# First expert layer: rest blocks of at most 64 rows get a TensorE unit of their own, in line ahead of the 128-row unit

## The chip, the cores and the metric

The kernel runs on one core of one Trainium2 chip. The metric is the device time in microseconds (us) from start to end of one execution; the median of the runs counts. Engines are named as the profile names them: PE is TensorE (PEld its weight loads), DVE is VectorE, ACT is ScalarE, POOL is GpSimd, SP is SyncE. A q behind an engine's name (PEldq, DVEq) stands for its instruction sequencer, which handles branches, registers and semaphore waits.

## What is computed

Retention attention, then two mixture-of-experts layers with one expert per token. Cut to what matters here:

```python
def _moe_ref(x, w_gate, w_output_gate, w1, w2):      # N, D, E, F = 4608, 512, 8, 1024
    e_idx = np.argmax(x @ w_gate, axis=1)
    for e in range(E):
        mask = e_idx == e
        h = np.maximum(x[mask] @ w1[e], 0.0)
        ye = h @ w2[e]
        out[mask] = gate_w[mask, None] * eom[mask, e, None] * ye

def reference(**kwargs):
    x = _attn_ref(q, k, v)                           # 8 x 8 heads, 576 rows, 64 wide
    x = _moe_ref(x, ...)                             # the first layer
    return _moe2_ref(x, ...)                         # the second, gated with a modality bias
```

On the inputs of the reference, its gate gives the eight experts of the first layer 602, 613, 589, 549, 586, 487, 608 and 574 rows. In the second layer two experts get all rows (2315 and 2293).

## The kernel before

Attention and routing of the first layer come first, in an order written out by hand (a plan sorted by numbers). The rows of each expert are scattered into a region of their own in DRAM. Then `experts` runs sixteen places in turn, 0 to 7 for the experts of layer one and 8 to 15 for those of layer two. Every engine has its own instruction stream, with branches on registers, and the streams meet only in semaphores: `take(engine, name)` waits for a semaphore and takes from it (its line in the profile is L547).

An expert's rows are worked in units. A unit of slot 0 or 1 is a pair, 256 rows. What is left is one rest unit (s = 2). The registers `np` (pairs) and `od` (the rest) are made in `counts` from the row count n of each expert: `np` is (n + 127) >> 8, and `od` was ((n + 127) >> 6) & 2, so 2 for a rest of 1 to 128 rows and 0 otherwise (a rest above 128 rows counts as a pair). By the counts above, every expert of layer one has two pairs; experts 0, 1, 2, 3, 4, 6 and 7 have a rest unit, with 90, 101, 77, 37, 74, 96 and 62 rows, and expert 5 has none.

What a unit does on each engine:

- PE, stage one (`quarter`, L1136 to L1138): four quarters of the hidden layer, 24 matmuls each, with the weights `w1` loaded and the rows `xT` moving. A pair moves 256 columns per matmul, a rest unit 128 (`cs = cols(P_, w)`). Each quarter gives `ph_full`.
- ACT (`relus`, L1264) makes the high half of `hT` from the quarter in `ph` and gives `hh_full`; DVE (`rests`, L1388) makes the low half and gives `h_full`.
- PE, stage two (`second`, L1144 to L1146): 24 matmuls per block of 128 rows, with `hT` loaded and 512 columns of `w2` moving. It takes `h_full` once before every six matmuls. `py_full` ends it.
- ACT and DVE (`back`): the squares and the scale of the block (`sq`, `eb`), then its two halves for the next layer (`x2row`). ACT and DVE run `back` of a unit before `relus` and `rests` of the next unit.
- Routing of the second layer runs one unit behind: PE's `logits` (L1114) and `ranks` (L1119, L1120), DVE's `choose` (the last step writes `oh`) and `place`. In a rest unit PE computes the logits of the previous pair's first block after six matmuls of stage two, and waits for `oh` at the end of stage two before the ranks.

The order within one expert of layer one is written by `walk`: the branches on `np` and `od` stand between the units. `co.jump(reg, op, value, target)` is a compare and branch that is taken to `target` or falls through; it has the line of the helper, L669. Branches inside units (`when`) have L648. After a rest unit comes `co.to(after)`, and then the next expert's first pair.

In layer two `walk` already chooses between a rest unit of 128 columns (`od` is 2) and one of 64 columns (`SMALL`, `od` is 1). `cols` gives a small unit of layer one the first 64 columns, and one of layer two the last 64.

## Time and profile before

| | |
|---|---|
| median of 3 runs | 987.47 us (987.39 to 988.93) |
| the profiled execution's own time | 986.25 us |
| its span, first to last instruction | 984.5 us |
| PE busy | 964.9 us, 98% of the span |
| DVE, ACT, POOL busy | 437.1, 353.8, 213.1 us |

The profiled execution takes 1.75 us beside its span and is 1.22 us below the median of the runs shown. A busy PE is one with a matmul in flight: a matmul's shown duration is longer than its distance to the next one, so pace is read from the starts of matmuls, and not from their durations.

### The profile page before, as it was taken

Reading aid. Unit: us, or ns where it says so; the run is one execution under the profiler, and the core shown is the slowest. Engines: PE = TensorE matmul, PEld = TensorE weight load, DVE = VectorE, ACT = ScalarE, POOL = GpSimd, SP = SyncE. Lnnn points to the kernel's source line nnn. Section 1 sums busy time; section 2 is a strip of 40 time slices with the busy share of each in tenths; the row PEclk is TensorE's granted clock in tenths of the full one; section 3 lists DMA queues with packets and bytes.
Section 4 is the critical chain, followed back from the end, with each engine's and each line's share of the span. In section 5 each row is a group of like instructions: output and inputs, shape, how many; then the busy total and the mean of one; then the engine's idle time right before and its main releaser. Section 6 shows DMA issues by size and latency. Waiting matters only on the chain. (4 is left out here: it accounts for less than half of the span.)

```text
span 984.5 us, 25261 instructions
## 1 busy us (share of the span) xinstructions
PE 964.9 (98%) x9218; PEld 684.2 (69%) x9218; DVE 437.1 (44%) x1402; ACT 353.8 (36%) x699; POOL 213.1 (22%) x301
## 2 busy tenths in 40 slices
PE   8999998999999999999999999999999999999997
PEld 6888887666676766767775776776666667766664
DVE  4676677366656565656566663243111211121111
ACT  4665565235444352434453432232111111211111
POOL 6677765011111111111111111100010101000110
PEclk9999999999999999999999999999999999999999
DMA  9999992578376664748664852642221311112101
GB/s 349 375 337 328 330 303 111 121 216 235 75 194 139 150 189 122 196 110 236 121 184 97 235 161 61 215 87 44 55 60 36 76 35 55 43 43 64 54 21 36
DMA packets 170070, 145.20 MB, mean 147 GB/s; under 512 B 135081, under 2 KB 135245, under 8 KB 169936
## 3 DMA queue, kind: packets, MB, share of 16 engines
q1 hardware_dynamic: 160928, 114.85, 43.0%
q0 software_dynamic: 8960, 28.62, 7.8%
q8 instruction: 73, 1.20, 0.5%
q14 instruction: 61, 0.50, 0.2%
q10 hardware_dynamic: 48, 0.04, 0.0%
HBM read 80.46 MB, written 33.92 MB: 116 GB/s over the span
## 5 line engine op out<-in xcount | busy, mean ns | idle before, releaser
L1138 PE MATMUL ph<-xT,wb 128*128 128x256 f16 (+2 forms) x1312 | 329.3, 262 | 0.0
L1137 PE MATMUL ph<-xT,wb 128*128 128x256 f16 (+2 forms) x1312 | 329.3, 262 | 0.0
L1136 PE MATMUL ph<-xT,wb 128*128 128x256 f16 (+2 forms) x1312 | 329.2, 262 | 0.0
L1388 DVE SCALAR_TENSOR_TENSOR hT<-ph,hT 128x512 f16<-128x512 f32 (+2 forms) x164 | 103.2, 636 | 322.0 <-DVEq L547 321.2
L1144 PE MATMUL py<-wb,hT 128*128 128x512 f16 x608 | 230.3, 379 | 0.1
L1146 PE MATMUL py<-wb,hT 128*128 128x512 f16 x608 | 230.4, 379 | 0.0
L1145 PE MATMUL py<-wb,hT 128*128 128x512 f16 x608 | 230.4, 379 | 0.0
L1264 ACT ACTIVATE hT<-ph 128x512 f16<-128x512 f32 (+2 forms) x164 | 90.1, 550 | 175.8 <-ACTq L547 175.6
L1136 PEld LDWEIGHTS ph<-xT,wb 128*128 128x128 f16 x1312 | 128.2, 98 | 15.6
L1137 PEld LDWEIGHTS ph<-xT,wb 128*128 128x128 f16 x1312 | 128.2, 98 | 15.4
L1138 PEld LDWEIGHTS ph<-xT,wb 128*128 128x128 f16 x1312 | 128.3, 98 | 12.2
L1146 PEld LDWEIGHTS py<-wb,hT 128*128 128x128 f16 x608 | 59.4, 98 | 71.8
L1551 POOL DMA_INDIRECT out_dram<-yo,idxo x37 | 35.9, 970 | 334.5 <-POOLq L547 324.7
L1144 PEld LDWEIGHTS py<-wb,hT 128*128 128x128 f16 x608 | 59.3, 98 | 64.3 <-issue 0.9
L1145 PEld LDWEIGHTS py<-wb,hT 128*128 128x128 f16 x608 | 59.4, 98 | 63.2
L559 DVE SCALAR_TENSOR_TENSOR wb<-stg,wb 128x2048 f16<-128x2048 f32 x36 | 82.4, 2288 | 10.0 <-DVEq L547 9.0
L1255 ACT ACTIVATE yo<-py,v_gcol 128x512 f32<-128x512 f32 x37 | 25.4, 687 | 167.5 <-ACTq L547 167.5
L1540 POOL TENSOR_SCALAR idx<-v_pos 128x1 int32<-128x1 f32 x39 | 9.1, 232 | 335.0 <-POOLq L547 335.0
L1238 ACT ACTIVATE wb<-stg 128x2048 f16<-128x2048 f32 x36 | 68.4, 1901 | 0.9 <-ACTq L547 0.9
L1249 ACT ACTIVATE sq<-py 128x512 bf16<-128x512 f32 x39 | 23.3, 596 | 93.4 <-ACTq L547 93.4
L1544 POOL DMA_INDIRECT xs<-x2row,idx x39 | 43.3, 1111 | 37.8 <-POOLq L547 36.5
L332 POOL TENSOR_SCALAR_AFFINE_SELECT a<-a 128x512 f32<-128x512 f32 x64 | 39.5, 641 | 26.2 <-ACT a L326 25.3
(165 smaller groups left out, 946.5 us busy)
## 6 DMA issues: line engine op xcount, KB each, us to landing
stg<-in_moe_w_dram SPq DMA_DIRECT2D x36, 1024.0 KB
dq<-in_dq_dram SPq DMA_DIRECT2D x34, 512.0 KB
vk<-in_vk_dram SPq DMA_DIRECT2D x30, 512.0 KB
w0s<-in_moe_w_dram SPq DMA_DIRECT2D x8, 512.0 KB
xs<-zero SPq DMA_DIRECT2D x8, 262.0 KB, 2.3
xs<-zero SPq DMA_DIRECT2D x8, 258.0 KB
vk<-in_vk_dram SPq DMA_DIRECT2D x8, 256.0 KB
gx<-in_scales_dram SPq DMA_DIRECT2D x5, 256.0 KB
```

The source lines that it names most:

```text
L332: nc.gpsimd.affine_select(out=d4, in_=d4, pattern=[[0, 4], [1, C]], compare_op=ALU.is_ge, fill=0.0, base=0, channel_multiplier=-1)
L559: r = fn(*a, **kw).then_inc(self.sem, 1)
L1136: pe.matmul(o, w1(P_, 0)[:, c, fs], xT[s][:, c, cs], start=(c == 0), stop=False)
L1137: pe.matmul(o, w1(P_, 0)[:, c, fs], xT[s][:, 4 + c, cs], start=False, stop=False)
L1138: m = pe.matmul(o, w1(P_, 1)[:, c, fs], xT[s][:, c, cs], start=False, stop=(c == 3))
L1144: pe.matmul(py[b], hT[:, 0, f, bs], w2(P_, 0)[:, f, :], start=(f == 0), stop=False)
L1145: pe.matmul(py[b], hT[:, 0, f, bs], w2(P_, 1)[:, f, :], start=False, stop=False)
L1146: m = pe.matmul(py[b], hT[:, 1, f, bs], w2(P_, 0)[:, f, :], start=False, stop=(f == 7))
L1238: ac.activation(wb[P_ % 2][:, 0, 2048 * c:2048 * c + 2048], stg[:, 2048 * c:2048 * c + 2048], AF.Copy, scale=WS).then_inc(T["cv_full"])
L1264: ac.activation(hT[:, 0, 2 * g:2 * g + 2, cs], ph[g][:, :, cs], AF.Relu).then_inc(T["hh_full"])
L1388: stt(hT[:, 1, 2 * g:2 * g + 2, cs], ph[g][:, :, cs], 0.0, hT[:, 0, 2 * g:2 * g + 2, cs], op0=ALU.max, op1=ALU.subtract).then_inc(T["h_full"])
L1544: po.indirect_dma_start(out=xs2, out_offset=bass.IndirectOffsetOnAxis(ap=idx[b], axis=0), in_=x, in_offset=None, bounds_check=E * R - 1, o ...
```

## The change

`counts` keeps two bits of the shifted count instead of one and takes one from them (with 0 kept): `od` is now 0 for no rest unit, 1 for a rest of 1 to 64 rows and 2 for 65 to 128. By the counts above experts 3 (37 rows) and 7 (62 rows) get 1; experts 0, 1, 2, 4 and 6 keep 2, and expert 5 keeps 0. All engines but PE still ask only whether `od` is 0, and do for 1 what they do for 2. PE alone is called with `short=True`.

```diff
         nc.vector.tensor_scalar(reg[:, 0:8], c2[:, 0], 8, None, op0=ALU.logical_shift_right)
-        nc.vector.tensor_scalar(reg[:, 8:16], c2[:, 0], 6, 2, op0=ALU.logical_shift_right, op1=ALU.bitwise_and)
+        nc.vector.tensor_scalar(c2[:, 0], c2[:, 0], 6, 3, op0=ALU.logical_shift_right, op1=ALU.bitwise_and)
+        nc.vector.tensor_scalar(reg[:, 8:16], c2[:, 0], 1.0, 1.0, op0=ALU.max, op1=ALU.subtract)
...
-    def walk(co, R_, P_, unit, none=None, conv=None, first=None, late=None, opening=None, owed=None):
+    def walk(co, R_, P_, unit, none=None, conv=None, first=None, late=None, opening=None, owed=None, short=False):
...
             unit(P_, 1, PAIR, True, 1)
-            co.to(block)
+            if short:
+                co.jump(od, "EQ", 0, after)
+                co.jump(od, "EQ", 2, block)
+                unit(P_, 2, SMALL, False)
+                eng.br(after)
+                co.at(block)
+            else:
+                co.to(block)
             if late:
                 co.unlikely(od, "EQ", 0, late, after)
             else:
                 co.jump(od, "EQ", 0, after)
             unit(P_, 2, FULL, False)
             co.to(after)
...
-                    walk(co, R_, P_, unit, none, opening=opening)
+                    walk(co, R_, P_, unit, none, opening=opening, short=True)
```

On PE, at the end of a pair of slot 1 (the last rows of its stage two), the program before goes on to one branch and the 128-column unit:

```order
L1144 MATMUL py<-wb,hT 128x512
L1145 MATMUL py<-wb,hT 128x512
L1146 MATMUL py<-wb,hT 128x512
L679 UNCONDITIONAL_BRANCH
L669 COMPARE_AND_BRANCH
L1136 MATMUL ph<-xT,wb 128x128
L1137 MATMUL ph<-xT,wb 128x128
L1138 MATMUL ph<-xT,wb 128x128
```

The changed program has at the same place two branches and the 64-column unit, whose matmuls have L1144 to L1146 in its own line numbers (stage two is L1152 to L1154 there):

```order
L1152 MATMUL py<-wb,hT 128x512
L1153 MATMUL py<-wb,hT 128x512
L1154 MATMUL py<-wb,hT 128x512
L670 COMPARE_AND_BRANCH x2
L1144 MATMUL ph<-xT,wb 128x64
L1145 MATMUL ph<-xT,wb 128x64
L1146 MATMUL ph<-xT,wb 128x64
```

So a 64-column unit is reached by falling through both branches, and a 128-column unit now by a taken branch that passes the whole 64-column unit.

At the end of the 64-column unit, behind the last matmuls of its stage two, the ranks and the register operation that notes the unit, the changed program leaves by a branch (L779) and has the 128-column unit behind it:

```order
L1154 MATMUL py<-wb,hT 128x512
L1127 MATMUL pr<-oh,tri 128x8
L1128 MATMUL pr<-cum,ones 128x8
L840 ISA
L779 UNCONDITIONAL_BRANCH
L670 COMPARE_AND_BRANCH
L1144 MATMUL ph<-xT,wb 128x128
L1145 MATMUL ph<-xT,wb 128x128
```

So a taken branch now stands between the end of a 64-column unit and the next expert, and it passes the 128-column unit: 140 matmuls with as many weight loads.

On DVE the counts get one more small operation on eight numbers, ahead of the low halves (L456) of the first unit, which is worked before the places begin. Before:

```order
L477 TENSOR_SCALAR c_3275<-cf 1x8
L478 TENSOR_SCALAR reg<-c_3275 1x8
L479 TENSOR_SCALAR reg<-c_3275 1x8
L456 SCALAR_TENSOR_TENSOR hT<-ph_early_3050,hT 128x512
L456 SCALAR_TENSOR_TENSOR hT<-ph_early_3194,hT 128x512
```

And now:

```order
L477 TENSOR_SCALAR c_3275<-cf 1x8
L478 TENSOR_SCALAR reg<-c_3275 1x8
L479 TENSOR_SCALAR c_3275<-c_3275 1x8
L480 TENSOR_SCALAR reg<-c_3275 1x8
L456 SCALAR_TENSOR_TENSOR hT<-ph_early_3050,hT 128x512
```

Nothing else moves on DVE, and no instruction is added, removed or moved on ACT, POOL and SP.

## Rows read from the trace of the kernel before

**Rows 1.** Busy time by engine, whole span.

```profile
PE 964.9 (98%) x9218; PEld 684.2 (69%) x9218; DVE 437.1 (44%) x1402; ACT 353.8 (36%) x699; POOL 213.1 (22%) x301
```

**Rows 2.** Groups by form, PE, 205 to 600 us: count, busy us, mean ns.

```profile
L1138 PE MATMUL ph<-xT,wb 128*128 128x128 f16 x224 | 37.9, 219 | 0.0
```

**Rows 3.** Timeline of PE, rest unit of expert 3: start us, duration us.

```profile
378.60 0.22 PE L1136 MATMUL ph<-xT,wb 128*128 128x128 f16 x1
...
383.96 0.38 PE L1144 MATMUL py<-wb,hT 128*128 128x512 f16 x1
...
389.39 0.27 PE L1136 MATMUL ph<-xT,wb 128*128 128x256 f16 x1
```

**Rows 4.** Timeline of PE, rest unit of expert 7.

```profile
583.17 0.22 PE L1136 MATMUL ph<-xT,wb 128*128 128x128 f16 x1
...
588.53 0.38 PE L1144 MATMUL py<-wb,hT 128*128 128x512 f16 x1
```

**Rows 5.** Timeline of PE, the 64-column unit of layer two.

```profile
782.05 0.19 PE L1136 MATMUL ph<-xT,wb 128*128 128x64 f16 x1
...
784.85 0.38 PE L1144 MATMUL py<-wb,hT 128*128 128x512 f16 x1
```

**Rows 6.** Timelines of ACT, then DVE, from the end of expert 3's second pair.

```profile
378.88 0.60 ACT L1249 ACTIVATE sq<-py 128x512 bf16<-128x512 f32 x1 [3.19 <-ACTq L547]
...
381.01 0.38 ACT L1264 ACTIVATE hT<-ph 128x256 f16<-128x256 f32 x1
...
381.33 0.74 DVE L559 SCALAR_TENSOR_TENSOR x2row<-py,v_s,x2row 128x512 f16<-128x512 f32 x1
382.75 1.12 DVE L1388 SCALAR_TENSOR_TENSOR hT<-ph,hT 128x256 f16<-128x256 f32 x3 [0.68 <-DVEq L547]
```

**Rows 7.** Timeline of DVE at expert 7's rest unit.

```profile
587.32 0.42 DVE L1388 SCALAR_TENSOR_TENSOR hT<-ph,hT 128x256 f16<-128x256 f32 x1 [0.67 <-DVEq L547]
```

**Rows 8.** PE's branches of `jump`: ns min/median/max, first and last start us.

```profile
L669 PEldq COMPARE_BRANCH  x15: 66/75/81, 209.9 to 460.4; - x15
...
L669 PEldq COMPARE_BRANCH  x2: 76/1595/3114, 481.8 to 485.1; - x2
...
L669 PEldq COMPARE_BRANCH  x1: 76/76/76, 387.9 to 387.9; - x1
```

**Rows 9.** PE's branches of `when`, leaving layer two's loops.

```profile
L648 PEldq COMPARE_BRANCH  x2: 75/219/363, 779.0 to 779.4; - x2
...
L648 PEldq COMPARE_BRANCH  x2: 348/1948/3547, 974.5 to 974.9; - x2
```

**Rows 10.** Timeline of PE, end of expert 5's second pair, start of expert 6.

```profile
485.43 0.38 PE L1146 MATMUL py<-wb,hT 128*128 128x512 f16 x1
485.64 0.27 PE L1136 MATMUL ph<-xT,wb 128*128 128x256 f16 x1
```

**Rows 11.** Timelines of PE and DVE at expert 1's first pair.

```profile
232.41 0.27 PE L1137 MATMUL ph<-xT,wb 128*128 128x256 f16 x1
232.52 0.27 PE L1138 MATMUL ph<-xT,wb 128*128 128x256 f16 x1
234.40 0.17 PE L1119 MATMUL pr<-oh,tri 128*128 128x8 f16 x1 [1.60 <-PEq L547]
...
233.91 0.29 DVE L559 TENSOR_SCALAR oh<-w_w,v_m,cur 128x8 f16<-128x8 f32 x1
```

**Rows 12.** Stretches: length, busy us of PE, PEld, DVE, ACT, POOL, granted clock, DMA.

```profile
235.90:239.40 3.50, 3.35 (x18) 2.12 (x16) 2.95 (x3) 1.06 (x1) 2.48 (x3) 0.51 1.01 391
...
8.00:12.00 4.00, 4.00 (x54) 2.85 (x54) 0.99 (x5) 1.47 (x3) 3.27 (x4) 1.00 1.03 389
```

**Rows 13.** Timeline of PE, a pause near the start.

```profile
7.93 1.16 PE L287 MATMUL pa<-dq 64*128 64x128 f32 x16 [2.15 <-DMA dq<-in_dq_dram]
```

**Rows 14.** Timeline of DVE at the counts.

```profile
173.13 0.15 DVE L479 TENSOR_SCALAR reg<-c 1x8 int32<-1x8 int32 x1
...
175.84 0.69 DVE L456 SCALAR_TENSOR_TENSOR hT<-ph_early,hT 128x512 f16<-128x512 f32 x1 [1.36 <-ACT hT L453]
```

## The prediction

> **What bounds the kernel now.** I read the page first, for the busy shares, and see PE busy for 98% of the span and no other engine above half [rows 1]. PE is the bound, so the question is what PE does in a rest unit, and what it would wait for if its part got shorter. Then the groups by form: 224 matmuls of 128 columns on each of three lines are seven rest units of layer one (32 per line and unit) [rows 2], as the row counts say. Two of these, experts 3 and 7, become 64-column units. Then I read PE's timeline at both. Stage one of expert 3's unit runs from 378.60 to 383.96, stage two and the rest of the unit until 389.39, where the next expert's pair starts [rows 3]; expert 7's stage one runs from 583.17 to 588.53 [rows 4]. In both it takes 5.36 us without a pause. So PE itself is what ends last in this stage, but how closely ACT and DVE follow has to be read from their own timelines.

> **Stage one gets shorter.** Layer two has one unit of 64 columns with the same 96 matmuls: 782.05 to 784.85, 2.80 us [rows 5]. The difference, 5.36 - 2.80 = 2.56 us, is what a short unit could give, 5.12 us for two.

> **What PE waits for then.** Stage two needs the first `h_full`, that is DVE's low half of the first quarter. DVE comes to it only behind `back` of the previous pair's second block, whose sums start when that pair's stage two has ended (378.60): ACT's squares at 378.88, its first high half at 381.01, DVE's `x2row` at 381.33, and the first low half at 382.75 [rows 6]. None of this depends on how long PE's stage one lasts, since quarter 0 was there long before, and DVE's order is not changed. A low half takes 0.42 us (the unmerged row at expert 7, [rows 7]), so the first is done at 383.17. From DVE's end to PE's start I take 0.20 us, from another place where PE stood waiting for DVE: `oh` ended at 233.91 + 0.29 = 234.20, and PE started at 234.40 [rows 11]. So stage two can start at 383.37 and not at 381.40, and the gain is 383.96 - 383.37 = 0.59 us. For expert 7 the low half starts at 587.32 [rows 7], so 587.32 + 0.42 + 0.20 = 587.94 against 588.53, again 0.59 us. Sum: 1.18 us faster. The bounds are a hand-over that costs nothing (0.79 us per unit) and one so late that today's start just meets it (0 us). I take 0.59, since PE's hand-over from the same engine is a direct row. The later three low halves follow 0.35 us apart or less (three in 1.12 us, [rows 6]) while stage two asks for one every six matmuls of 0.22 us [rows 10], so they hold nothing up. Stage two and its routing move as they are: the logits are PE's own, and `choose` follows them.

> **The branches.** Fifteen of PE's `jump` branches up to expert 5's pairs, all of which fell through, took 66 to 81 ns. The one that skipped expert 5's missing unit took 3114 ns [rows 8]. It cost nothing on the array: PE's sequencer was at that branch at 481.8 while matmuls already issued ran until 485.64, where the next pair started on pace, 0.21 us behind the last one [rows 10]. The cover was 3.84 us. Skips out of layer two's loops took 363 ns (779.0), 348 ns (974.5) and 3547 ns (974.9) [rows 9]. So of four taken skips of about a unit's length two were dear; I take one chance in two, and 3.11 us as the price.

> [...]

> Five long units (experts 0, 1, 2, 4, 6) now start with a taken branch past the short unit, at the same place as expert 5's skip, with the same cover of 3.84 us. One more branch of 0.08 us stands ahead. I take 0, up to 0.43 us each if a fetch is as slow as the 3547 ns row (2.2 us for five). Expert 5's skip gets longer; I take it as dear as before and as well hidden.

> The return from a short unit has less cover. It stands just ahead of the next expert's branch, which PE's sequencer reached at 387.9 [rows 8], because it had to wait for `oh` before the ranks. The next pair started at 389.39 [rows 3], so the lead was 1.5 us. At expert 6 the same branch at 485.1 [rows 8] was followed by its pair at 485.64 [rows 10], so at most 0.54 us of the lead is needed and at least 0.95 us is slack. A dear return then loses 3.11 - 1.5 = 1.6 to 3.11 - 0.95 = 2.2 us; I take 1.9. A cheap one loses nothing. Two returns at one chance in two: one dear is the likeliest.

> **The operation on DVE.** About 0.15 us like its neighbours. Behind it DVE sat idle for 1.36 us, waiting for ACT [rows 14]; that idle time hides it. Without it, it would cost its 0.15 us.

> **Sum.** -1.18 + 1.9 = +0.7 us against the profiled execution's own 986.25, so 987.0; the same against the median, 987.47, which lies 1.22 above it: **988.2 us**. I count 0.2% (2.0 us) as what a measurement of this kernel can tell from no change, so this is no change.

> **The rivals.**
> - Both returns cheap: only the 1.18 us remain, 986.3 us. For it: the two cheap skips. Against it: expert 5's skip has the same length.
> - Both returns dear: -1.18 + 3.8 = +2.6, 990.1 us. [...]
> - The clock falls, and this one ends slower: PE stands still in each short unit from 378.60 + 2.80 = 381.40 to 383.37, 1.97 us. [...] Two units: 2 x (1.7 - 0.59) = +2.2, 989.7 us. It decides from the first fall of the clock behind a short unit's pause; one fall alone gives +0.5. Against it: a pause near the start, 2.15 us until 7.93 [rows 13], was followed by full clock from 8 to 12 [rows 12], so a pause of this length need not bring a fall. A slow stage two would also cover part of a dear return, so I don't add them.
> - The whole 5.12 us: 982.3 us. It needs low halves that are ready at 381.4. Against it stands DVE's row at 382.75, for which I see no way around.

> **How the numbers follow.** One return dear 0.40 (988.2); both cheap 0.19 (986.3); both dear 0.17 (990.1); the clock falls 0.18 (989.7); the whole gain 0.04 (982.3); long units pay for their skips 0.02 (up to 990.4 with the likeliest case). Faster by over 0.2%: the whole gain and a little for the noise, 0.06. Within: the first two, 0.58 after the noise. Slower: both dear, the clock and the long units, 0.36. The range reaches from both cheap with the gain's upper bound (987.47 - 2 x 0.79 = 985.9) to both dear (990.1, with some room 990.3). The likeliest case's own range, with returns of 1.6 to 2.2 and gains of 0 to 0.79 per unit, is 987.5 to 989.7.

> **What would show it.** Two lots of 96 matmuls of 128x64 in layer one, in 2.8 us each. Behind each a pause on PE of about 2 us, ended by DVE, with stage two starting about 4.8 us behind the pair's end, not 5.36. The `jump` branches of five long units at about 3 us or 75 ns with PE on pace behind them either way. Behind each short unit, either PE on pace or a gap of some 1.9 us before the next expert's first matmul. The granted clock at 1.00 in the 5 us behind each pause. I would be wrong if DVE's first low half came earlier than 4.1 us behind the pair's end, if the clock fell, or if a pause appeared ahead of a long unit.

## The result, and the profile after

| | before | after |
|---|---|---|
| median, us | 987.43 (6 runs) | 997.38 (6 runs) |
| profiled execution, us (its span) | 986.25 (984.5) | 998.05 (996.2) |

The changed kernel takes 1.0101 of the time before (95% interval 1.0091 to 1.0112). That is slower by 10 us, outside the predicted range.

PE stays the bound. This is the line of engines on the page of the kernel after, beside [rows 1]; the second line is the instruction queue q8 from the page's third part (packets, MB, share), which had 73 packets before. (The other instruction queue, q14, has 61 packets in both kernels; it is PE's program that grew, so q8 is taken to be PE's.)

```profile
PE 966.5 (97%) x9218; PEld 682.7 (69%) x9218; DVE 437.1 (44%) x1403; ACT 353.0 (35%) x699; POOL 212.2 (21%) x301
...
q8 instruction: 80, 1.31, 0.6%
```

PE is busy for only 1.6 us more in a span that is 11.7 us longer: the short units take work off it, something puts work time back on, and the rest is standing still. The timeline of PE after, at expert 3's short unit and the start of expert 4's first pair, answers to [rows 3]:

```profile
378.82 0.19 PE L1144 MATMUL ph<-xT,wb 128*128 128x64 f16 x1
...
381.60 0.19 PE L1146 MATMUL ph<-xT,wb 128*128 128x64 f16 x1
383.54 0.38 PE L1152 MATMUL py<-wb,hT 128*128 128x512 f16 x1 [1.75 <-PEq L548]
...
388.97 0.27 PE L1144 MATMUL ph<-xT,wb 128*128 128x256 f16 x1
...
389.30 0.27 PE L1144 MATMUL ph<-xT,wb 128*128 128x256 f16 x1
393.74 0.37 PE L1145 MATMUL ph<-xT,wb 128*128 128x256 f16 x1 [4.17 <-issue]
```

Up to 388.97 this is the forecast: stage one in 2.8 us, a pause of 1.94 us, stage two 4.72 us behind the unit's start in place of 5.36. Then the next pair starts on pace, does four matmuls, and stands still for 4.33 us beyond its pace. "issue" says that PE waited for nothing that the profile shows: no semaphore, no engine, no transfer of data. DVE's timeline has the first low half where the first step put it, 4.15 us behind the unit's start ([rows 6] had 4.15):

```profile
382.97 1.45 DVE L1396 SCALAR_TENSOR_TENSOR hT<-ph,hT 128x256 f16<-128x256 f32 x4 [0.68 <-DVEq L548]
```

At expert 7 the gap stands in front of the pair that follows, and is put down to PE's sequencer (beside [rows 4]):

```profile
590.78 0.19 PE L1144 MATMUL ph<-xT,wb 128*128 128x64 f16 x1
...
593.55 0.19 PE L1146 MATMUL ph<-xT,wb 128*128 128x64 f16 x1
595.72 0.38 PE L1152 MATMUL py<-wb,hT 128*128 128x512 f16 x1 [1.98 <-PEq L548]
...
601.12 0.17 PE L1128 MATMUL pr<-cum,ones 128*128 128x8 f16 x1
604.21 0.27 PE L1144 MATMUL ph<-xT,wb 128*128 128x256 f16 x1 [2.92 <-PEq L548]
```

The branches of PE's sequencer after, beside [rows 8]: the two returns (ns min/median/max, first and last start), then `jump` at expert 5's and expert 6's unit.

```profile
L779 PEldq COMPARE_BRANCH  x2: 281/2295/4309, 387.3 to 599.4; - x2
...
L670 PEldq COMPARE_BRANCH  x1: 4071/4071/4071, 488.5 to 488.5; - x1
...
L670 PEldq COMPARE_BRANCH  x2: 66/1736/3406, 532.9 to 533.0; - x2
```

Expert 7's return took 4309 ns. Expert 3's took 281 ns and looks harmless; its price stands four matmuls later. Over 387.2 to 391.2 us the transfers show no packet of the instruction queue, over 391 to 393 us one:

```profile
q8 instruction: 1, 0.02, 3.0%
```

So no packet was moving while PE worked off the first four matmuls, and PE goes on 1.5 us behind the end of that packet (it ran from 391.31 to 392.27).

The clock comes on top. Stretches of PE after, beside [rows 12] (length, busy us of PE, PEld, DVE, ACT, POOL, granted clock, DMA share, GB/s): behind expert 3's pause, behind expert 3's return, behind expert 7's pause, behind expert 7's return.

```profile
383.50:388.50 5.00, 4.96 (x31) 2.37 (x32) 2.33 (x10) 0.60 (x3) 0.00 (x0) 1.00 0.88 173
392.90:399.70 6.80, 5.96 (x36) 4.30 (x36) 0.92 (x5) 0.84 (x3) 0.00 (x0) 0.50 0.83 249
...
595.70:600.70 5.00, 4.98 (x31) 2.38 (x31) 2.49 (x10) 0.60 (x3) 0.00 (x0) 1.00 0.59 125
604.55:607.90 3.35, 3.35 (x18) 2.41 (x16) 0.00 (x0) 0.00 (x0) 0.00 (x0) 0.50 1.02 139
```

The granted clock stays at 1.00 behind both pauses and is 0.50 behind both returns. In the second stretch PE was busy for 5.96 us; by the starts of its matmuls the clock of 0.50 cost 2.8 us of them.

The account, by the starts of the same stages in the two traces:

| place | us against before |
|---|---|
| up to expert 3's unit | +0.2 |
| the two short units (pause included) | -0.65, -0.42 |
| return from expert 3: the gap, and the clock behind it | +4.3, +2.8 |
| expert 5's skip, now over two units | +0.7 |
| experts 6 and 7, small waits | +0.2 |
| return from expert 7: the gap, and the clock behind it | +3.1, +1.7 |
| sum | +11.9 |

The sum is that of the two profiled executions, of which the one before lies 1.2 us below its kernel's median and the one after 0.7 us above; between the medians it is 10 us.

### The profile page after: what moved, and what is told of

Same layout as the page of the kernel before. It is cut to its first block, busy times and chain, and to the rows that moved or that the text cites. A ratio compares the mean times of both kernels' runs of the same rounds, so it can differ in the third digit from the quotient of the medians.

```text
span 996.2 us, 25276 instructions
## 1 busy us (share of the span) xinstructions
PE 966.5 (97%) x9218; PEld 682.7 (69%) x9218; DVE 437.1 (44%) x1403; ACT 353.0 (35%) x699; POOL 212.2 (21%) x301
## 5 line engine op out<-in xcount | busy, mean ns | idle before, releaser
L1144 PE MATMUL ph<-xT,wb 128*128 128x256 f16 (+2 forms) x1312 | 326.4, 262 | 3.4 <-PEq L548 3.4
L1146 PE MATMUL ph<-xT,wb 128*128 128x256 f16 (+2 forms) x1312 | 326.5, 262 | 0.0
L1152 PE MATMUL py<-wb,hT 128*128 128x512 f16 x608 | 230.3, 379 | 3.7 <-PEq L548 3.7
L1154 PE MATMUL py<-wb,hT 128*128 128x512 f16 x608 | 230.4, 379 | 0.0
L1144 PEld LDWEIGHTS ph<-xT,wb 128*128 128x128 f16 x1312 | 128.3, 98 | 20.3 <-issue 4.2
L1146 PEld LDWEIGHTS ph<-xT,wb 128*128 128x128 f16 x1312 | 128.4, 99 | 17.3 <-issue 4.3
L1154 PEld LDWEIGHTS py<-wb,hT 128*128 128x128 f16 x608 | 59.4, 98 | 71.8
L1152 PEld LDWEIGHTS py<-wb,hT 128*128 128x128 f16 x608 | 59.3, 98 | 67.7 <-issue 4.3
L1548 POOL TENSOR_SCALAR idx<-v_pos 128x1 int32<-128x1 f32 x39 | 7.1, 181 | 347.0 <-POOLq L548 347.0
```

The costliest lines, as they stand in the source:

```text
L1144: pe.matmul(o, w1(P_, 0)[:, c, fs], xT[s][:, c, cs], start=(c == 0), stop=False)
L1146: m = pe.matmul(o, w1(P_, 1)[:, c, fs], xT[s][:, c, cs], start=False, stop=(c == 3))
L1152: pe.matmul(py[b], hT[:, 0, f, bs], w2(P_, 0)[:, f, :], start=(f == 0), stop=False)
L1154: m = pe.matmul(py[b], hT[:, 1, f, bs], w2(P_, 0)[:, f, :], start=False, stop=(f == 7))
```

## The experiments

Theory A: the loss is a wait for instructions behind the short units' return, where nothing covers it, and the clock that falls behind that gap. Rival B: the pause for `h_full` drags the clock down. Rival C: the skips ahead of the long units cost it. The two kernels with fixed units hold the widths of experts 3 and 7 for the counts of this input alone. The absolute times in the first four expectations start from 987.4 us; beside these runs the kernel before took 983.62 us, so it is the differences that are compared. There is one trace of each kernel.

### Short units in place, fixed when the program is built

```diff
-            unit(P_, 2, FULL, False)
+            unit(P_, 2, SMALL if short and P_ in (3, 7) else FULL, False)
```
(and no unit in front of it)

> Experts 3 and 7 get the 64-column unit when the kernel is built (these inputs' counts), in place of the long one; no branch is added and no code is skipped. Theory A (the loss is the wait for instructions behind the return from a short unit, and the clock that falls after it): a pause of about 1.95 us in each short unit stays, no gap behind it, no fall of the clock behind it; 1.2 us under the kernel before, 986.3 us. Rival B (the pause for the first low half is what makes the clock fall): the clock falls behind the pauses as it does in the changed kernel, 3 to 5 us lost, 989 to 991 us. Rival C (the skips ahead of the long units cost the time): as A, no loss.

Measured: 981.64 against 983.62 us, 0.9983 (0.9973 to 0.9992). PE at expert 3, then the stretches behind both pauses:

```profile
378.67 0.19 PE L1139 MATMUL ph<-xT,wb 128*128 128x64 f16 x1
380.62 0.38 PE L1145 MATMUL py<-wb,hT 128*128 128x512 f16 x1 [1.75 <-PEq L548]
...
380.60:385.60 5.00, 4.98 (x31) 2.40 (x32) 2.31 (x10) 0.59 (x3) 0.00 (x0) 1.00 0.90 165
584.70:589.70 5.00, 4.97 (x31) 2.40 (x32) 2.52 (x10) 0.60 (x3) 0.00 (x0) 1.00 0.55 114
```

The same pause, and the clock stays at 1.00: B falls. Without branches the short columns are a gain, and of the size that the prediction gave them (1.18 us of the sum; here 1.7, interval 0.8 to 2.7, and in the trace 0.65 us at each of the two units).

### The copy alone: the unit in front does 128 columns too

```diff
-                unit(P_, 2, SMALL, False)
+                unit(P_, 2, FULL, False)
```

> The branches and the code of the change, but the unit in front works 128 columns like the long one, so that nothing gets shorter and PE doesn't pause for the first low half. Theory A: the returns of experts 3 and 7 each cost a gap of 3 to 4.4 us, and some falls of the clock remain: 5 to 10 us over the kernel before, 993 to 997 us. Rival B: without the pause the clock doesn't fall and the loss is at most the 3 us of one return, 987 to 991 us. Rival C: the whole loss is there, 997 us.

Measured: 993.69 against 983.62 us, 1.0114 (1.0095 to 1.0132). PE behind the two returns:

```profile
386.04 0.27 PE L1144 MATMUL ph<-xT,wb 128*128 128x256 f16 x1
389.92 0.37 PE L1145 MATMUL ph<-xT,wb 128*128 128x256 f16 x1 [3.61 <-issue]
...
596.88 0.17 PE L1128 MATMUL pr<-cum,ones 128*128 128x8 f16 x1
599.91 0.27 PE L1144 MATMUL ph<-xT,wb 128*128 128x256 f16 x1 [2.87 <-PEq L548]
```

No column is saved and no pause is left, and the whole loss is there, with the granted clock at 0.50 from 389.29 and from 600.91 for 3.4 us each. The layout alone (1.0114) and the columns alone (0.9983) multiply to 1.0097, beside 1.0101 for both. The loss belongs to the program's layout, not to the narrower unit. It is 10.1 us, at the upper end of A's 5 to 10 and as much as C expects, so its time speaks against B alone; its trace puts 9.7 us at the two returns, and the next run settles C.

### Skips only: every rest unit long, the copy in front never entered

```diff
-        nc.vector.tensor_scalar(reg[:, 8:16], c2[:, 0], 1.0, 1.0, op0=ALU.max, op1=ALU.subtract)
+        nc.vector.tensor_scalar(reg[:, 8:16], c2[:, 0], 2, None, op0=ALU.bitwise_and)
```

> The short unit's code stands in line, but the rest register is made as before (0 or 2), so all seven rest units are long and are reached by the taken branch past the short one; nothing returns over code but expert 5's skip of both units. Theory A: the branches of 2 to 4 us stand under matmuls already issued, expert 5's skip shows 0.7 us: 987.4 to 988.5 us. Rival B: the same. Rival C: most of the loss is here, 993 to 997 us.

Measured: 984.68 against 983.62 us, 1.0013 (1.0002 to 1.0024). All of it stands at expert 5, whose skip now passes two units (4416 ns):

```profile
483.56 0.38 PE L1154 MATMUL py<-wb,hT 128*128 128x512 f16 x1
484.78 0.27 PE L1144 MATMUL ph<-xT,wb 128*128 128x256 f16 x1 [0.85 <-PEq L548]
```

C is worth 1.0 us, and A expected up to 1.1. The long units' own skips, up to 3431 ns, left PE on pace.

### The long unit in front, the short one behind it

```diff
-                co.jump(od, "EQ", 2, block)
-                unit(P_, 2, SMALL, False)
+                co.jump(od, "EQ", 1, small)
+                unit(P_, 2, FULL, False)
                 eng.br(after)
+                co.at(small)
+                unit(P_, 2, SMALL, False)
...
```

> The long unit stands in front of the short one: five long units fall in and return over the short unit's code, two short units are reached by a taken branch and run on into the next expert. Theory A: five returns instead of two, each 3 to 4.4 us and some with a fall of the clock of 1.7 us: 15 to 28 us over the kernel before, 1002 to 1015 us. Rival B: the two pauses cost what they do in the changed kernel, 994 to 998 us. Rival C: two skips instead of five, under 992 us.

Measured: 998.91 against 983.62 us, 1.0157 (1.0131 to 1.0182). Now five long units return over the short one. PE's five returns, and the gaps behind those of experts 1, 2, 4 and 6:

```profile
L781 PEldq COMPARE_BRANCH  x5: 390/417/6397, 222.9 to 549.7; - x5
...
286.88 0.28 PE L1150 MATMUL ph<-xT,wb 128*128 128x256 f16 x1 [1.05 <-issue]
...
341.03 0.28 PE L1148 MATMUL ph<-xT,wb 128*128 128x256 f16 x1 [1.25 <-issue]
...
450.27 0.37 PE L1148 MATMUL ph<-xT,wb 128*128 128x256 f16 x1 [5.02 <-PEq L548]
...
553.72 0.27 PE L1148 MATMUL ph<-xT,wb 128*128 128x256 f16 x1 [2.52 <-PEq L548]
```

The kernel is 15.3 us above the one before, just inside A's 15 to 28 but not by A's count of five dear returns: three of five took some 0.4 us, and two of these three were followed by an "issue" gap 2 to 3 us into the next pair. Two were dear, with a fall of the clock at each, and expert 5's skip lost 1.2 us. The short units, which return from nowhere here, have no gap behind them. A branch's own duration does not tell its price.

### Low halves early: can the pause go?

The fixed short units again. Besides, ACT and DVE do the unit's first two high and low halves inside the eviction of the pair's last block.

```diff
+                        if held:
+                            back(1, 1, lambda: some(range(2), False))
...
                     ch(ve.reciprocal, v1["inv2"][b], v1["rinv2"][b])
+                    if between:
+                        between()
                     take(ve, "x2h_full")
```
(and the same on ACT, between `sq` and the high half of `x2row`)

> The short units of experts 3 and 7 sit in the place of the long ones, fixed when the program is built, as in the run with the static units (0.9983 of the time before); besides, ACT and DVE do the first two high and low halves of these two units inside the eviction of the pair's last block, where they waited for each other, and not behind it. If the pause of PE in a short unit (1.84 us lost, twice) is only the late first low half, as the sum's first step has it, it is gone: stage two follows stage one on pace, and the run is 2 x 1.84 = 3.7 us faster than the static units, about 5.1 us (0.9948) faster than before. The rival: the eviction's later half, pushed back, is what the next wait is for (the routing of the block, or the buffer that the next pair needs), and the pause moves instead of going: about 0.9983 again, with a new gap of 1 to 2 us behind the unit.

Measured: 981.69 against 986.72 us, 0.9952 (0.9938 to 0.9966). PE around the start of stage two, then DVE:

```profile
381.70 0.19 PE L1139 MATMUL ph<-xT,wb 128*128 128x64 f16 x1
381.98 0.38 PE L1145 MATMUL py<-wb,hT 128*128 128x512 f16 x1
...
381.21 0.76 DVE L1406 SCALAR_TENSOR_TENSOR hT<-ph,hT 128x256 f16<-128x256 f32 x2
...
381.94 0.74 DVE L560 SCALAR_TENSOR_TENSOR x2row<-py,v_s,x2row 128x512 f16<-128x512 f32 x1
```

The first low halves stand ahead of `x2row`, stage two starts 0.28 us behind stage one, and no wait comes in its place. The whole gain is real: 4.7 us (0.9952 of 986.72), where the prediction worked out 5.12. This is also a second run of PE's program of the fixed short units, and expert 5's skip took 3057 ns where it took 3054: the same program showed the same branch time in two traces.

### One stage two for both widths

```diff
...
+                co.jump(od, "EQ", 2, wide)
+                unit(P_, 2, SMALL, False, part=1)
+                eng.br(both)
+                co.at(wide)
+                unit(P_, 2, FULL, False, part=1)
+                co.to(both)
+                unit(P_, 2, FULL, False, part=2)
...
```

> Only stage one of a rest unit exists twice; both widths go on into one common stage two, with its routing, so that nothing returns from a short unit into the next expert. A short unit branches in its middle, over the long stage one, where PE then stands still for DVE for 1.95 us anyway; a long unit skips the short stage one at its head, where 3.84 us of matmuls are queued. Theory A (the loss is the instruction wait behind the return, uncovered, and the clock behind the gap): no gap at the next experts' first pairs, at most a longer pause in the middle of the short units (a wait of 3 to 4.3 us less a cover of about 2.4: 0.6 to 1.9 us each); 0.999 to 1.003 of the time before, with a fall of the clock only if a pause reaches some 3 us. The rival (any short unit reached by a branch costs what the change cost): 1.010 again.

Measured: 988.16 against 986.72 us, 1.0014 (1.0005 to 1.0023). PE inside expert 3's short unit, and behind expert 5's skip (5462 ns):

```profile
383.70 0.38 PE L1158 MATMUL py<-wb,hT 128*128 128x512 f16 x1 [1.76 <-PEq L548]
...
487.39 0.27 PE L1150 MATMUL ph<-xT,wb 128*128 128x256 f16 x1 [1.89 <-PEq L548]
```

No return into the next expert, and no gap there. A branch of 1767 ns in the middle of expert 3's short unit was hidden under its pause. Both short units gain 0.65 us; expert 5's skip takes 2.06 us back. A held, in its range.

### The short unit out of line, at the end of PE's program

```diff
+                co.unlikely(od, "EQ", 1, lambda: unit(P_, 2, SMALL, False), after)
```
(in place of the unit in front)

> The short units stand far behind, at the end of PE's program; the long ones stay in line with no branch around them other than the old skip where there is no rest, and one more branch that falls through. Theory A by distance (what is not just ahead in the program must be fetched, however far): the jump out is covered by the queued matmuls (3.84 us), or loses up to 0.5 us, and the two returns into the next experts lose 3 to 4.3 us each and a fall of the clock each as in the changed kernel: 1.008 to 1.011 of the time before, and expert 5's skip back to what it cost before. The rival (the price hangs on the length of the code that is jumped over): the far jumps cost more than in the changed kernel, over 1.011, with gaps over 5 us.

Measured: 991.12 against 986.72 us, 1.0043 (1.003 to 1.0056). PE in the two short units:

```profile
378.96 0.19 PE L1139 MATMUL ph<-xT,wb 128*128 128x64 f16 x1
382.78 0.19 PE L1140 MATMUL ph<-xT,wb 128*128 128x64 f16 x1 [3.62 <-issue]
...
588.31 0.20 PE L1139 MATMUL ph<-xT,wb 128*128 128x64 f16 x1 [2.20 <-issue]
```

Both theories missed. The jumps out (3632 and 4068 ns) were followed by gaps of 3.8 and 2.4 us inside the short units, which swallowed the pauses; behind the second the clock fell (0.50 from 589.2 to 592.6), for 0.8 us more. Both returns, over far more code, cost nothing on PE. So distance alone does not make a return dear; two returns are too few to say more. Expert 5's skip went back to 2913 ns and was hidden again.

### Work added as cover: 16 matmuls of 512 columns ahead of the return

```diff
+                    if w == SMALL and P_ < E:
+                        for n in range(16):
+                            pe.matmul(ph[3], K["ones"], K["ones"].unsqueeze(1).to_broadcast([P, 4, P]), start=True, stop=True)
```

> The changed kernel with work added: 16 matmuls of 512 columns on constants (16 x 0.21 = 3.4 us) at the end of each short unit, ahead of its return, into sums that nobody reads any more. Theory A: they are the cover that the return lacked, so that the gaps in front of the next experts' pairs (4.3 and 3.0 us) shrink to 1 us or less and the clock no longer falls behind them (it cost 2.8 and 1.7 us): the two places cost 2 x 3.4 in place of 11.9 us, and the kernel with more work is 4 to 5 us faster than the changed one, 1.005 to 1.006 of the time before. The rival (the wait starts only when PE gets to the next pair, or comes from something else than the return): the gaps stay as they are and the kernel is 6.8 us slower than the changed one, about 1.017.

Measured: 1004.06 against 986.72 us, 1.0172 (1.0157 to 1.0188). That is the rival's number, but not by the rival's mechanism. PE behind expert 3's return, the stretches behind both returns, and then expert 6's first pair, behind expert 5's skip:

```profile
395.92 0.27 PE L1144 MATMUL ph<-xT,wb 128*128 128x256 f16 x1 [1.50 <-PEq L548]
...
395.90:400.90 5.00, 4.98 (x52) 4.51 (x53) 1.25 (x6) 1.19 (x4) 0.00 (x0) 1.00 0.86 231
611.70:616.70 5.00, 4.96 (x52) 4.50 (x53) 1.25 (x6) 1.19 (x4) 0.00 (x0) 1.00 0.86 103
...
494.26 0.27 PE L1144 MATMUL ph<-xT,wb 128*128 128x256 f16 x1 [1.86 <-PEq L548]
...
498.68 0.37 PE L1144 MATMUL ph<-xT,wb 128*128 128x256 f16 x1 [3.60 <-issue]
```

At the returns A's mechanism is there: with the added work included they cost 5.1 and 3.9 us, against 7.1 and 4.7 without it, the gaps shrink to 1.7 and 0.5 us (A had 1 or less), and the clock stays at 1.00. The loss moved elsewhere. Expert 5's skip, which passes a longer unit (5434 ns), lost 2.0 us, then 3.8 us more inside the pair, then the clock: 7.2 us in place of 0.7. Some 1.9 us more stand ahead of the first rest unit, where no theory has a claim. The total alone would have told the wrong story.

### PE's program shifted by 128 and by 64 instructions

```diff
+                        if (P_, slot, at) == (0, 1, 5):
+                            with when(pe, was, "EQ", 7):
+                                for n in range(64):
+                                    pe.matmul(ph[3], K["ones"], K["ones"].unsqueeze(1).to_broadcast([P, 4, P]), start=True, stop=True)
```
(range(32) in the second; the branch around them is always taken)

How much of a packet that is, is an estimate from the trace of the kernel before: from 16.2 to 161.4 us it has 22 packets of q8 with 0.36 MB, and 2715 matmuls with 2711 weight loads on PE, so 16.4 KB and 247 of these instructions to a packet, some 66 bytes each, and 128 are about half a packet.

> The changed kernel, with 64 matmuls that are never executed (128 instructions with their weight loads, half of a 16 KB packet of the instruction queue at 64 bytes each) behind a branch in expert 0's second pair, so that all of PE's program behind them lies half a packet further, and nothing else differs. Theory A, as it now stands (an instruction wait comes where PE's sequencer, behind a taken branch, comes to the end of what has been fetched): the same branches are at other distances from the packets' ends, so that the places and the sizes of the gaps change: the 4.3 us gap one matmul behind expert 3's return is gone or elsewhere, and the time differs from the changed kernel's by over 2 us, anywhere between 0.998 (no gap) and 1.017. The rival (the price of a return is fixed by the branch and its distance): the same gaps at the same places, 1.010 within 0.002.

> As the run before it, with 32 matmuls that are never executed: a quarter of a packet. Theory A: again other places and sizes, between 0.998 and 1.017, and of the two shifted kernels at least one differs from the changed one by over 2 us. The rival: 1.010 within 0.002.

Measured: 995.67 and 994.53 against 986.43 us, 1.0106 (1.009 to 1.0122) and 1.0081 (1.0068 to 1.0094). Returns and the gaps behind them, by 128, then by 64 (in the changed kernel the gap behind expert 3's return lies four matmuls in, not one as the expectation has it):

```profile
L779 PEldq COMPARE_BRANCH  x2: 339/3276/6213, 385.1 to 599.6; - x2
...
391.78 0.37 PE L1144 MATMUL ph<-xT,wb 128*128 128x256 f16 x1 [4.84 <-PEq L548]
...
604.00 0.27 PE L1145 MATMUL ph<-xT,wb 128*128 128x256 f16 x1 [2.21 <-issue]
```

```profile
L779 PEldq COMPARE_BRANCH  x2: 437/3077/5717, 386.5 to 600.3; - x2
...
392.63 0.29 PE L1144 MATMUL ph<-xT,wb 128*128 128x256 f16 x1 [4.34 <-PEq L548]
```

The places changed as A said: expert 3's return became the dear one (6213 and 5717 ns where it took 281), in front of the pair and not four matmuls into it, and expert 7's became cheap, with a gap four matmuls in or (by 64) none at all. The time did not change as A said: neither kernel moved by clearly more than 2 us against 1.0101. The rival had the time (1.010 within 0.002) and missed the places. What one place gives, another takes: expert 5's skip lost 2.1 and 1.9 us where it lost 0.7, and besides, by 128, 1.4 us inside the pair behind it, and by 64, 1.1 us inside expert 6's long unit, which stands behind a skip of 3316 ns. So the place in the program decides which return pays and in which form, but this did not amount to a way out.

### The kernel before, and the common stage two, shifted by 128

The same four lines in each.

> The kernel before, shifted by half a packet in the same way. It has one taken skip in layer one, expert 5's. Theory A: at most that skip's price changes, between hidden and some 2 us at the pair behind it: 0.999 to 1.002, and up to 1.004 if the clock falls behind it. The rival: 1.000 within 0.001.

> The kernel with the common stage two (1.0014 where it stood), shifted by half a packet. It lost 2.06 us behind expert 5's skip and gained 0.6 and 0.4 us at the short units. Theory A: the skip's loss and the wait in the middle of the short units change with the place; with all of it hidden it would be 0.999, with a gap in the middle of both short units as large as behind the returns (4.3 less the 2.0 us that PE stands there anyway) 1.005 or more. The rival: 1.0014 within 0.001.

Measured: 986.30 against 986.43 us, 1.0000 (0.9991 to 1.0009); and 991.03 us, 1.0056 (1.0037 to 1.0074). Expert 5's skip in the kernel before, shifted, and in the common stage two PE at expert 5 and expert 7:

```profile
L669 PEldq COMPARE_BRANCH  x2: 76/200/325, 480.2 to 480.8; - x2
```

```profile
489.81 0.28 PE L1151 MATMUL ph<-xT,wb 128*128 128x256 f16 x1 [2.48 <-issue]
...
591.43 0.57 PE L1158 MATMUL py<-wb,hT 128*128 128x512 f16 x1 [2.23 <-PEq L548]
```

The kernel before does not care where it stands: its one skip went from 3114 to 325 ns, and both are under its cover; its time fits A and the rival alike. The common stage two does: the same code 128 instructions further lost 4 us, with a gap of 2.6 us inside the pair behind expert 5's skip, and a clock that fell behind expert 7's pause of 2.4 us.

## Why the prediction was wrong

- **The pause and the gain: right.** 1.97 us were forecast, 1.94 and 2.17 measured; 0.59 us per unit were forecast, 0.65 and 0.42 measured, and 0.65 at each with the fixed units, whose whole gain was 1.7 us where the sum had 1.18.
- **The five long units: right.** Their skips took up to 3406 ns and PE stayed on pace behind them, as the cover of 3.84 us said. Each of the two dear skips of the kernel before had one packet of q8 under it (one over 481.8 to 485.0 us, one over 974.9 to 978.5).
- **DVE's operation: right.** It shows nowhere.
- **The return: the step that failed.** "Two returns at one chance in two: one dear is the likeliest", at 1.9 us. Both were dear, 4.3 and 3.1 us, and the clock behind them took 2.8 and 1.7 us more: 11.9 us where the sum had 1.9. Three things were off: the price, the chance and the form. The price of a dear branch: 4.31 us at expert 7, where the sum took 3.11 from expert 5's skip. (The lead was sized well: PE reached that return at 599.45 for a pair due at 601.15, 1.7 us, where 1.5 were taken; 0.45 us of it were needed, and 4.31 - 1.7 + 0.45 is the 3.06 us lost.) The chance: of the 13 returns into a next expert that were run with no cover added (the changed kernel, the copy, the long unit in front, the two shifts), nine lost 2.4 to 5.2 us, two lost 1.2 to 1.4, two lost nothing. And the form: "a cheap one loses nothing" did not hold, since a return of 281 ns was followed by 4.3 us of waiting four matmuls on. The page of the profile lists that gap as "issue", and the kernel before has none over 0.6 us. The case of both returns dear, which came true, had a chance of 0.17 and 990.1 us, at the same price of 1.9 us each. Behind expert 3's return, from 387.2 to 391.2 us, the trace has no packet of the instruction queue, and the stall came four matmuls behind the branch.
- **The clock: right rival, wrong place.** The text tied the fall to the `h_full` pause, and said of a dear return and a fall "I don't add them". The clock held behind both pauses and fell behind both gaps, for 2.8 and 1.7 us more. A gap and the clock behind it belong together in one case of the forecast. The price of a fall in that case's sum, 1.7 us, is the author's estimate from expert 1's first pair in the kernel before: 16 weight loads in the 3.5 us at a clock of 0.51 ([rows 12]), so about 16 matmuls of 256 columns, at the 0.11 us from start to start that these take ahead of its pause ([rows 11]). It came true at expert 7's return, but not in that place: in the kernel with the unit out of line the clock held at expert 1's first pair, and PE, there early, waited 1.9 us; stage two started at 239.38, where it starts at 239.37 in the kernel before. So that fall cost nothing.
- **Expert 5's skip: small, but off.** "As dear as before and as well hidden": over twice the code it took 4071 ns, more than the cover of 3.84 us, and 0.7 us showed. In all nine kernels whose skip passes more than one unit's code it took 4.1 to 5.5 us and PE lost 0.7 to 2.1 us in front of the pair (and in three of them 1.4 to 3.8 us more inside it); in the five where it passes one unit it took 0.3 to 3.1 us and PE lost nothing.
- **The whole gain: possible after all.** "I see no way around" DVE's row at 382.75: the order of ACT and DVE can be changed, and then the time is 0.9952 of that before.

What stays open: what exactly decides whether a return is cheap, since the places moved with a shift of the program, but no rule was derived that tells them beforehand; whether the transfers of data have a part in the size of the price (below), since no run changed them alone; and why the clock fell behind some gaps and not behind others of the same length (below).

## What to carry to other kernels

On a bound engine, code that a run does not execute is not free: a taken branch cost up to 5.2 us of standing still here, at the branch or a few instructions behind it, so put it where more than that is queued, and look for "issue" gaps and not only for long branches. Before a variant with a branch is built, time its two halves apart, once with the saving and no branch and once with the branch and no saving; here that gave 0.9983 and 1.0114. And before columns are cut, see who the engine waits for next: the larger half of this saving lay in the order of the two engines behind it.
